# Weights loaded by halves of the heads and token transposes as column tiles, in a planned two-layer kernel

## The chip, the cores and the metric

The kernel runs on one core of one Trainium2 chip. The metric is the device time of one execution in microseconds. TensorE (PE in the profile) multiplies, ScalarE (ACT) does exponentials and copies, VectorE (DVE) does copies, statistics and a second kind of exponential, GpSimd (POOL) does small vector work, and SyncE (SP) issues the DMAs, all in one queue.

## The reference

Two blocks alternate, twice each, with the same weights: attention, then a mixer over the tokens.

```python
x = x + A(layernorm(x), wqkv, wo)            # 2048 tokens, width 640, 32 heads of 20
x = x + B(layernorm(x), w1, b1, w2, b2)      # a token MLP: 2048 -> 1536 -> 2048
x = x + A(layernorm(x), wqkv, wo)
x = x + B(layernorm(x), w1, b1, w2, b2)

def A(x, wqkv, wo):
    qkv = (x @ wqkv).reshape(B, S, 3, H, Dh).transpose(2, 0, 3, 1, 4)
    q, k, v = qkv[0], qkv[1], qkv[2]
    p = softmax(einsum("bhqd,bhkd->bhqk", q, k) * Dh ** -0.5)
    return einsum("bhqk,bhkd->bhqd", p, v).transpose(0, 2, 1, 3).reshape(B, S, D) @ wo

def B(x, w1, b1, w2, b2):
    u = gelu(einsum("bsd,sf->bdf", layernorm(x), w1) + b1)
    return (einsum("bdf,fs->bds", u, w2) + b2).transpose(0, 2, 1)
```

The layernorms have no learned scale. Inputs, weights and output are bfloat16.

## The kernel before

**Units of attention.** Heads are taken in 8 groups of four; a group's four heads sit at partitions 0, 32, 64 and 96 of the padded weights `wq` and `wk` (32 columns a head, 20 of them used), of `KT` (keys, transposed, 2048 columns a group) and of `QT` (512 queries of a group). A unit is one group, one block of 512 queries and one tile of 128 keys. Its scores are four matmuls that use 32 rows of the array each (`s_mms`, L700). ACT takes the exponential of two or three 512-column banks at once (L887, into `P`); for some units DVE does it instead with integer arithmetic (L840 and five passes of L860, into `JT`). The sums with V are matmuls with 32 columns of the array each, four side by side (L927, out of `P` or `JT`, with `Vaug`, which also holds a column of ones for the denominators).

**From x to Q, K and V.** `token_tile` takes one of 16 tiles of 128 tokens: statistics on DVE (L343 to L346), the scale on POOL (L354, L356), the normalised tile `h_bf` on DVE (L530, three buffers in the region of `attnT`), five 128x128 transposes on TensorE (L541, into a bfloat16 bank), and a copy into `hT` (region `hh`) by ACT or DVE (`copy`, L461 or L463). When four tiles are there, the projections of K and Q for 512 tokens can run (`add_proj`), and V's for each tile (`add_v`, half of the heads at a time). Every projection is a "fill": a list of matmuls that the planner puts between scores and sums. Outside attention these matmuls use the whole array (L453); within attention `mmul` issues each as four column tiles (L456), so that they stand next to the sums with V without a change of tiling. The transposes use the whole array at all times.

**Weights.** At the start `front` issues four token tiles, Q's weights, K's weights (800 KB each, region `JT`), two more token tiles, V's weights (800 KB, in the region `attnT`), and the other ten token tiles, for which eight slots exist. `pad_copies` spreads Q's and K's weights into the padded `wq` and `wk`, five copies of 128x640 each, on whichever of ACT and DVE is free. A projection may start when all five copies of its matrix are done. The second layer keeps `wq` and `wk` and loads V's weights again when the first layer's attention outputs are dead (`on_attnT_dead`).

**Order of attention.** The first layer takes groups 0 to 3 of the first 512 queries first, over key tiles 0 to 3 and then 4 to 15, as tokens come; then groups 4 to 7, then the other query blocks. The second layer takes key tiles four at a time, as the mixer of the first layer (`add_mm2`) gives out new tokens. The very last unit group (last query block, last head group) is taken in two halves of 256 queries, so that the output projection of the first half runs beside the second.

**Normalising.** After a group's sums are done, `normalize` turns them in 32x32 blocks on DVE (L977), takes reciprocals (L989), multiplies (L1000, on POOL, for the very last half on DVE) and turns them back (L1007). L1007 works on pairs of 16-bit values as 32-bit elements; the multiply writes the pairs in the order that needs, and `outproj` (L1059) reads its queries with the matching stride.

**The planner.** The whole program is one hand-written order. At build time the Python code simulates the five queues (`clk`) with estimated costs (`PE_MM`, 64 ns for a transpose, `PAD_V` for a pad copy on DVE, `DMA_RATE`, `SW` = 100 ns for a change of tiling on TensorE) and appends the cheapest ready instruction to each engine. The order on each engine is then fixed; on the chip semaphores keep it right, and an instruction that waits holds everything behind it on its engine. `fill_mode` tells the planner whether a fill runs in column tiles or on the whole array.

## Time and profile before

| what | value |
|---|---|
| median of 3 runs | 1728.17 us (1724.88 to 1728.33) |
| the profiled execution's own time | 1728.33 us |
| its span on the core | 1726.6 us |
| PE busy | 1643.3 us, 95% |
| ACT busy | 1583.5 us, 92% |
| DVE busy | 1458.4 us, 84% |
| POOL busy | 171.8 us, 10% |
| granted TensorE clock, mean | 0.997 |
| first layer's attention | 16 to 797 us |
| second layer's attention | 839 to 1652 us |

Times in the rows are in microseconds from the span's start, durations in microseconds on timeline rows and in nanoseconds for the mean of a group. A timeline row merges neighbours of one engine with the same line and tiles: start, length, engine, line, operation, written and read tiles, shape, how many, and in square brackets the idle time before it with what ended it. Matmuls are pipelined, so that a row of one matmul is longer than the distance to the next; distances between starts are what counts. `PEld` are weight loads. Lines named L461 and L463 belong to `copy`, L453 and L456 to `mmul` and L276 to `dma`, so their tiles tell which of them is meant.

### The profile page before, as it was taken

The page shows a single profiled execution, that of the slowest core. Times are in us where ns is not written, and L with a number is a line of the kernel's source. Part 1 is how long each engine was busy: PE and PEld are TensorE (multiplying, and loading weights), DVE is VectorE, ACT ScalarE, POOL GpSimd, SP SyncE. Part 2 cuts the span into 40 slices and gives each one's busy share as a digit, 9 for nine tenths or more (in the row PEclk, how much of TensorE's full clock was granted, in tenths as well). Part 3 has the DMA queues.
Part 4 walks back from the last instruction along what each step waited for, and adds up shares of the span by engine and source line. Part 5 has one row for each costly group of instructions (what it writes and reads, how often), then busy time and mean ns, then how long its engine had stood idle before and what let it go on. Part 6 is the DMA issues. An engine that isn't in the chain of part 4 may idle for free. (4 is left out here: it accounts for less than half of the span.)

```text
span 1726.6 us, 50507 instructions
## 1 busy us (share of the span) xinstructions
PE 1643.3 (95%) x21918; PEld 640.3 (37%) x21918; DVE 1458.4 (84%) x2620; ACT 1583.5 (92%) x1431; POOL 171.8 (10%) x260
## 2 busy tenths in 40 slices
PE   8999999999999999998999999999999999999989
PEld 3433333223333333335545432333333333332356
DVE  7688999999988898998444589999999889999973
ACT  8899999999999999997698899999999999999950
POOL 4000012000300020001101000100002000200010
PEclk9999999999999999999999999999999999999999
DMA  3200001000122016411521000100002120365142
GB/s 119 29 2 2 2 14 36 1 1 2 52 70 70 25 43 206 155 40 38 160 85 67 16 2 2 40 24 2 2 17 71 58 65 24 95 195 181 40 129 91
DMA packets 103294, 98.05 MB, mean 57 GB/s; under 512 B 45600, under 2 KB 79520, under 8 KB 103072
## 3 DMA queue, kind: packets, MB, share of 16 engines
q1 hardware_dynamic: 99456, 94.82, 17.8%
q8 instruction: 171, 2.80, 0.7%
q0 software_dynamic: 3616, 0.01, 0.3%
q14 instruction: 51, 0.42, 0.1%
HBM read 63.35 MB, written 31.46 MB: 55 GB/s over the span
## 5 line engine op out<-in xcount | busy, mean ns | idle before, releaser
L887 ACT ACTIVATE P<-pst 128x1536 bf16<-128x1536 f32 (+1 forms) x1337 | 1521.7, 1320 | 30.9 <-PE pst L700 17.0
L860 DVE TENSOR_SCALAR JT<-JT 128x2048 uint16<-128x2048 uint16 x945 | 633.9, 700 | 4.8 <-PE pst L927 1.6
L700 PE MATMUL pst<-QT,KT 32*128 32x512 bf16 (+1 forms) x4224 | 573.3, 376 | 44.5 <-ACT P L887 32.4
L840 DVE TENSOR_SCALAR JT<-pst 128x512 uint16<-128x512 f32 x756 | 504.2, 677 | 77.5 <-PE pst L700 75.8
L927 PE MATMUL pst<-P,Vaug 128*32 128x512 bf16 (+1 forms) x3444 | 509.1, 381 | 3.2 <-DVE T_85 L977 1.8
L927 PE MATMUL pst<-JT,Vaug 128*32 128x512 bf16 (+1 forms) x3900 | 470.8, 380 | 3.0 <-DVE T_85 L977 1.6
L700 PEld LDWEIGHTS <-KT 32*128 32x128 bf16 x4224 | 169.1, 91 | 515.7 <-issue 502.4
L927 PEld LDWEIGHTS <-Vaug 128*32 128x32 bf16 x7344 | 168.9, 94 | 295.2 <-issue 262.9
L1000 POOL TENSOR_TENSOR T_86<-T_85,rden 128x512 bf16<-128x512 f32 x64 | 67.7, 1059 | 1145.9 <-DVE rden L989 1106.1
L1481 PE MATMUL pst<-ident,zw 128*32 128x512 bf16 (+1 forms) x347 | 113.5, 380 | 0.0
L456 PEld LDWEIGHTS <-W 128*32 128x32 bf16 x3384 | 88.5, 96 | 64.6 <-issue 31.9
L1059 PE MATMUL pst<-wo,attnT 128*32 128x320 bf16 x2048 | 106.0, 301 | 3.9 <-DVE attnT L1007 2.9
L456 PE MATMUL pst<-hh,wq 128*32 128x512 bf16 x1232 | 104.6, 382 | 1.5 <-DVE JT L840 1.2
L456 PE MATMUL pst<-hh,wk 128*32 128x512 bf16 x1240 | 96.8, 381 | 1.3 <-DVE JT L840 0.6
L456 PE MATMUL pst<-x1last,W 128*32 128x320 bf16 x1536 | 78.9, 301 | 1.0 <-DVE W L1245 0.4
L1059 PEld LDWEIGHTS <-attnT 128*32 128x32 bf16 x2048 | 52.2, 96 | 38.8 <-issue 18.2
L456 PE MATMUL pst<-attnT,hh 128*32 128x320 bf16 x1196 | 60.2, 300 | 2.0 <-DVE hh L463 0.7
L456 PE MATMUL pst<-JT,W 128*32 128x320 bf16 x1080 | 52.3, 300 | 0.0
L463 DVE CAST KT<-pst 128x512 bf16<-128x512 f32 x52 | 35.3, 680 | 18.6 <-PE pst L456 18.4
L456 PE MATMUL pst<-hh,W 128*32 128x320 bf16 x768 | 42.8, 304 | 7.8 <-DMA W<-in_B_w_dram 4.5
L977 DVE STREAM_TRANSPOSE T_85<-pst 128x512 f32<-128x512 f32 (+1 forms) x58 | 40.0, 689 | 8.0 <-PE pst L927 7.9
L463 DVE CAST Vaug<-pst 128x320 bf16<-128x320 f32 x43 | 20.5, 482 | 30.4 <-PE pst L456 21.7
(91 smaller groups left out, 851.8 us busy)
## 6 DMA issues: line engine op xcount, KB each, us to landing
W<-in_B_w_dram SPq DMA_DIRECT2D x10, 768.0 KB
W<-in_B_w_dram SPq DMA_DIRECT2D x24, 256.0 KB
xs<-in_A_x_dram SPq DMA_DIRECT2D x32, 160.0 KB
x2d<-xs SPq DMA_DIRECT2D x16, 320.0 KB
xs<-x2d SPq DMA_DIRECT2D x16, 320.0 KB
x1d_69<-xs SPq DMA_DIRECT2D x12, 320.0 KB
uacca_72<-W SPq DMA_DIRECT2D x12, 320.0 KB
W<-uacca_72 SPq DMA_DIRECT2D x12, 320.0 KB
```

What stands on the lines that cost most here:

```text
L456: nc.tensor.matmul(out_[32 * c:32 * c + 32], lhsT=lhsT[:, 32 * c:32 * c + 32], rhs=rhs, start=start, stop=stop, tile_position=(0, 32 * c))
L463: nc.vector.tensor_copy(out=out_, in_=in_)
L700: pe(nc.tensor.matmul(dst, lhsT=k_, rhs=q_, start=True, stop=True, tile_position=(32 * j, 0)))
L840: nc.vector.tensor_scalar(out=c["jt"][:, j * 512:(j + 1) * 512], in0=Dt[:], scalar1=SCALE * LOG2E * 256.0, scalar2=127.0 * 256.0, op0=ALU. ...
L860: nc.vector.tensor_scalar(out=tt_[:], in0=c["jt"][:], scalar1=0.5, scalar2=TERM_C[i], op0=ALU.mult, op1=ALU.add)
L887: nc.scalar.activation(out=P[:, 0:n, :].rearrange("p a b -> p (a b)"), in_=St[:, 0:n, :].rearrange("p a b -> p (a b)"), func=ACT.Exp, scal ...
L927: pe(nc.tensor.matmul(dst, lhsT=Vaug[:, n:n + 32], rhs=ap, start=acc["cnt"][j] == 1 and not part, stop=last[j] and (half is None or part = ...
L977: nc.vector.transpose(out=T1[:], in_=src[:, 0:w])
L1000: eng.tensor_tensor(out=o_, in0=a_, in1=b_, op=ALU.mult)
L1059: nc.tensor.matmul(t[32 * c:32 * c + 32, 0:w], lhsT=q_, rhs=wo_pad[:, gg, c0:c1], start=(gi == 0), stop=(gi == len(gs) - 1), tile_position ...
L1481: pe(nc.tensor.matmul(dst[0:32, 0:128 * n], lhsT=zw[:, 0:32], rhs=ident[:].unsqueeze(1).to_broadcast([128, n, 128]), start=not inside, sto ...
```

## The change

- Q's, K's and V's weights are loaded in two halves, the first for heads 0 to 15 and the second for heads 16 to 31 (400 KB each, rows of 640 bytes). Q and K have four places in the region `JT`, V two in `attnT`. The first halves of Q and K are issued where the whole ones were, V's first half after token tile 5; the second halves get a lower priority on SP than token tiles that are ready.
- Q and K are padded by halves: 20 copies of 128x320 instead of 10 of 128x640. A projection waits for the half that its head group is in, and V's projection of one half for that half of V's weights. The second layer's V weights come in two loads as well.
- Within attention each transpose of a 128x128 block of normalised tokens becomes four, of 32 columns each, at column tiles 0, 32, 64 and 96. The planner treats them as column tiles.
- For the two halves of the last head group, the turning back works on 256 16-bit elements instead of 128 32-bit ones; the multiply writes in plain order, and the output projection of that group reads without the stride. All other groups stay as they were.
- Planner's costs: a pad copy on DVE 260 instead of 450, on ACT 460 instead of 730; the turning back 340 instead of 70 + 0.56 ns a query; the weight loads' rates.

```diff
-PAD_V = 450.0
+PAD_V = 260.0
...
-    at("wraw", "JT", 0, NDT * D * 2)
+    at("wraw", "JT", 0, NDT * D)
...
-    at("wv", "attnT", 0, NDT * D * 2)
+    at("wv", "attnT", 0, NDT * D)
...
-        return "col" if COL_FILL and not f["bf16"] and a is not None and a.want and not a.done else "full"
+        return "col" if COL_FILL and a is not None and a.want and not a.done else "full"
...
-            if t > start and t + f["cost"] + (SW if state.col or f["bf16"] else 0.0) > s_at[0] + FILL_OVER:
+            if t > start and t + f["cost"] + (SW if state.col else 0.0) > s_at[0] + FILL_OVER:
...
-        def load_wv():
-            L.wv = sb("wv", [128, NDT, D], BF16)
-            dma(L.wv[:], A_wqkv[:, 2 * D:3 * D].rearrange("(dt p) n -> p dt n", p=128), 128 * NDT * D * 2,
-                then=lambda t: setattr(L, "wv_ready", t))
+        def load_wv(hf):
+            L.wv[hf] = sb("wv", [128, NDT, D // 2], BF16, hf)
+            c0, c1 = COLS[hf]
+            dma(L.wv[hf][:], A_wqkv[:, 2 * D + c0:2 * D + c1].rearrange("(dt p) n -> p dt n", p=128), 64 * NDT * D * 2,
+                prio=1 + hf, rate=DMA_RATE * 0.8, then=lambda t: L.wv_ready.update({hf: t}))
...
-                        pe(nc.tensor.transpose(t[:, dt_, :], h_bf[:, dt_ * 128:(dt_ + 1) * 128], ident[:]))
+                        if state.col:
+                            for c in range(4):
+                                nc.tensor.transpose(t[32 * c:32 * c + 32, dt_, :], h_bf[:, dt_ * 128 + 32 * c:dt_ * 128 + 32 * c + 32], ident[:],
+                                                    tile_position=(0, 32 * c))
+                        else:
+                            nc.tensor.transpose(t[:, dt_, :], h_bf[:, dt_ * 128:(dt_ + 1) * 128], ident[:])
...
-            add_fill(mms, PE_MM, evac, 600.0, ready=ready, pr=pr, ok=lambda: w_left[what] == 0 and (what == "K" or len(rQ) > 0),
+            add_fill(mms, PE_MM, evac, 600.0, ready=ready, pr=pr, ok=lambda: w_left[(what, g // 4)] == 0 and (what == "K" or len(rQ) > 0),
...
-                            nc.vector.transpose(out=attnT[(qb, g)][:, q0:q1].bitcast(F32), in_=T2[:].rearrange("p c i -> p (c i)").bitcast(F32))
+                            o_, i_ = attnT[(qb, g)][:, q0:q1], T2[:].rearrange("p c i -> p (c i)")
+                            if half is None:
+                                o_, i_ = o_.bitcast(F32), i_.bitcast(F32)
+                            nc.vector.transpose(out=o_, in_=i_)
...
-            if L.nxt:
-                L.nxt.load_wv()
+            if L.nxt:
+                for hf in range(2):
+                    L.nxt.load_wv(hf)
...
-                copy(eng, w_view(wpad, dt_)[:, :, 0:DH], wr[:, dt_, :].rearrange("p (h i) -> p h i", i=DH))
+                copy(eng, w_view(wpad, dt_)[:, h0:h1, 0:DH], wr[:, dt_, :].rearrange("p (h i) -> p h i", i=DH))
...
-            either.append((1.5, t, seq[0], PAD_V, 730.0, f))
+            either.append((1.5 if hf == 0 else 2.5, t, seq[0], PAD_V, 460.0, f))
...
-        load_w(1)
-        load_w(0)
+        load_w(1, 0)
+        load_w(0, 0)
         for tt in range(4, 6):
             load_x0(tt)
-        L0.load_wv()
+        L0.load_wv(0)
         for tt in range(6, NT):
             load_x0(tt)
+        load_w(1, 1)
+        load_w(0, 1)
+        L0.load_wv(1)
```

## The prediction

> **What bounds the kernel now.** I read the page's first two parts, then the busy time in stretches of 20 us, then the timeline at three places: the first 17 us, the first layer's token stage to 80 us, and the second layer's token stage from 840 to 955 us. The page says that no engine is idle for long:
>
> ```profile
> PE 1643.3 (95%) x21918; PEld 640.3 (37%) x21918; DVE 1458.4 (84%) x2620; ACT 1583.5 (92%) x1431; POOL 171.8 (10%) x260
> L1481 PE MATMUL pst<-ident,zw 128*32 128x512 bf16 (+1 forms) x347 | 113.5, 380 | 0.0
> ```
>
> TensorE's 95% is an average with filler in it: L1481 is a matmul on zeros that only keeps the clock up, 113.5 us in all. Where those stand, TensorE has room; none stands between 16 and 40 us, and next to none in the second layer's token stage. So I look at the stages that the change touches one by one. First the start:
>
> ```profile
> 10.66 1.70 PE L453 MATMUL pst<-hh,wq 128*128 128x512 bf16 x7 [0.25 <-ACT hh L461]
> 9.29 0.72 ACT L461 COPY wq<-JT 128x640 bf16<-128x640 bf16 x1 [0.30 <-DMA JT<-in_A_wqkv_dram]
> 13.59 0.58 ACT L461 CAST KT<-pst 128x512 bf16<-128x512 f32 x1 [0.22 <-PE pst L453]
> 14.72 0.57 PE L453 MATMUL pst<-attnT,hh 128*128 128x320 bf16 x3 [1.17 <-DMA attnT<-in_A_wqkv_dram]
> 16.42 0.39 PE L700 MATMUL pst<-QT,KT 32*128 32x512 bf16 x3
> ```
>
> Q's weights land at about 9.2 us, but Q's projection starts at 10.66 when the fourth tile of normalised tokens is there. Keys are cast by 14.17. The first scores come only at 16.42: in TensorE's order a V projection stands ahead of them, and that one waits 1.17 us for V's weights, which land at 14.7.
>
> Then who waits for whom in the token stage of the first layer:
>
> ```profile
> 20.00:40.00 20.00, 19.13 (x257) 7.09 (x257) 14.96 (x37) 18.79 (x18) 6.82 (x14) 1.00 0.12 35
> 40.00:60.00 20.00, 19.66 (x282) 8.36 (x280) 9.62 (x21) 19.51 (x18) 4.59 (x3) 1.00 0.53 60
> 65.08 0.58 ACT L461 CAST KT<-pst 128x512 bf16<-128x512 f32 x1 [1.05 <-PE pst L456]
> 75.86 0.58 ACT L461 CAST KT<-pst 128x512 bf16<-128x512 f32 x1 [1.30 <-PE pst L456]
> ```
>
> The first two rows give PE, PEld, DVE, ACT, POOL. PE is full; ACT, which does the exponentials, catches up with the projections at 65 and 76 us and waits for keys. So this stage ends when TensorE's work ends, and what counts is TensorE's time, not ACT's first exponential. The second layer's token stage is the same: PE has 10.0 of 10 us from 840 to 860, and ACT waits 3.73 us at 908.9 and 3.94 us at 947.4 for the transposes of a new block of tokens. Their surroundings:
>
> ```profile
> 62.14 0.59 PE L456 MATMUL pst<-attnT,hh 128*32 128x320 bf16 x12
> 62.67 0.45 PE L541 MATMUL pst<-ident,attnT 128*128 128x128 bf16 x5
> 63.05 0.50 PE L927 MATMUL pst<-P,Vaug 128*32 128x512 bf16 x4
> 905.26 3.17 PE L456 MATMUL pst<-JT,W 128*32 128x320 bf16 x85
> 908.86 1.99 ACT L461 COPY hh<-pst 128x640 bf16<-128x640 bf16 x3 [3.73 <-PE pst L541]
> 912.91 1.26 PE L456 MATMUL pst<-hh,wk 128*32 128x512 bf16 x20
> ```
>
> Five whole-array transposes start (0.45-0.22)/4 = 0.057 us apart (one lasts 0.219). Going from column tiles into them costs about 0.53 - 3x0.137 = 0.12 us, leaving them about 0.38 - 5x0.057 = 0.095 us; 0.1 us a crossing.
>
> **Weights by halves (first layer).** Bytes come in order. Summing the DMA rates in half-microsecond slices from the start (56, 282, 300, 251, 274, 207, 177, 276, then some 364 GB/s), the 1,475 KB of four token tiles and Q's weights have moved at 7.0 us and are seen at 9.2: a lag of 2.2 us. By the same sums Q's half (1,065 KB) has moved at 5.9 and is seen at 8.1, K's half at 9.2 instead of 11.4, V's half (2,212 KB, two more token tiles before it) at 11.2 instead of 14.7. Rows of 640 bytes in place of 1,280 could slow this; the nearest row, w2's 512-byte rows at 344 to 351 GB/s from 1652 to 1660 us, makes it 5%, V's half at 11.5. It is then there before TensorE asks for it at 13.4: minus 1.17 us. ACT's pad copies of Q come ahead of its copies of the transposed tokens, for the half now lands as ACT is done with its memsets (8.13): four copies of 320 columns at 0.43 (the 128x320 cast's row) where one of 0.72 stood, which I take to delay the last token copy by 0.3 us; against it, TensorE's waits for wq copies of 0.28 and 0.22 us go. Taken: minus 1.2 us. Bounds: 0, if another wait, for the token copies, fills the hole; minus 2.25, if the first scores follow the key cast at once (16.42 - 14.17).
>
> The second halves: ten more pad copies, 0.16 to 0.32 us each on DVE (row: 0.32 for 640 columns), 2 to 3 us that fall on DVE between 15 and 60 us, where it is busy under 75%; on ACT they would be ten times 0.43. Cover gone, they cost ACT's share, 2 us. SP issues three more DMAs, 0.5 us each (two took 1.00). Ahead of token tile 8 stand 3,280 KiB instead of 3,680 KiB, so no token comes later; its issue waits for a free slot till 7.5 us anyway. POOL's queue is not touched. In the second layer V's load is issued at 799.60 and first used at 828.5: one more issue of 0.38 us on a queue that next issues at 818.7. Nothing.
>
> **Transposes as column tiles.** 120 of the 160 transposes lie within attention, 60 in each layer, in pieces between other matmuls. Counting pieces that follow or precede column-tile matmuls without another wait between, I find 12 crossings in the first layer and 8 in the second: 20x0.1 = minus 2.0 us, all in stages where TensorE is the bound. The row that the trace does not have is four transposes of 32 columns side by side with 128 moving columns. Column-tile groups of four run 0.137 us apart at 320 columns and (1.26-0.38)/4 = 0.22 at 512: both give 0.055 at 128 in proportion, which is also the whole-array row. I take 0.057: no change. The other end is that a group never goes faster than at 320 columns: 120x(0.137-0.057) = plus 9.6 us. That bound also holds for 480 instructions in place of 120, should their issue set the pace.
>
> A rule of the Trainium skill speaks against this edit. TensorEngine Tiling (Array Packing), "Restrictions" under Tile-to-Partition Mapping, says that column tiling disables the fast weight load, and TensorE: Matmul & The Clock Gate, "LDWEIGHTS (loading the stationary operand)", puts a load at columns/1.2 ns. An estimate from that page is 107 ns for four loads of 32 columns, and with it this term would be plus 4.0 us instead of minus 2.0; no row of this trace shows loads as the limit.
>
> **The last head group in 16-bit elements.** The second halves' transposes (L1007, 0.31 us for 128x128 32-bit) are on the path at both layers' ends; 128x256 16-bit elements cost between 0.31 and the 0.43 of the 128x256 32-bit row. Taken 0.43: 2x0.12 = plus 0.25 us, bounds 0 and 0.25. The multiply ahead of it keeps its 256 elements (0.44). The first halves lie beside POOL and other head groups.
>
> **Planner's costs** (PAD_V, 340 for the turning back) move the order, not the work.
>
> Sum: -1.2 - 2.0 + 0.25 = -2.95. The profiled execution took 1728.33 us (span 1726.6), 0.16 above the median of 1728.17: 1725.4.
>
> **Rivals.**
> 1. Slower: column-tile transposes are paced by their instructions or weight loads, not by 128 columns. For: 8 instructions a group, a pace that the trace never shows. Against: at 512 and 320 columns the pace is proportional. At 0.137 us a group the time is 1725.4 + 9.6 = 1735.0; from 0.11 us on it is over 0.2% slower than before.
> 2. Nothing reaches the end: TensorE's order has other waits (0.59 us at 18.7 for a V cast, ACT's casts at 65) that take up the gains, and only the +0.25 is left: 1728.6. Against: PE is full in the windows.
> 3. A larger gain: the new order also brings one of the two token blocks in time (the 3.73 us wait), and the start keeps 2.25 instead of 1.2: 1725.4 - 3.7 - 1.0 = 1720.7. For: the waits are just after TensorE's full stretch. The same re-planning the other way, one wait more, gives 1729.2, with a second 1733.
>
> **How the numbers follow.** Forecast 0.38, its own range 1723.5 to 1727.5; larger gain 0.23; nothing reaches the end 0.10; slow tiles 0.20; a worse order 0.09. About 0.2%, 3.5 us, is what a measurement of this kernel can tell from no change, so faster means under 1724.7 and slower over 1731.6. Two fifths of the forecast's chance (0.15) and the larger gain are faster: 0.38. Nearly all of the slow tiles (0.19) and over half of the worse order (0.06) are slower: 0.25. Same has the other 0.37. The range runs from the larger gain to the milder slow tiles and the worse order: 1720.5 to 1733.
>
> **What would show it.** First V projection without a wait on its weights and first scores near 15.2 us; ACT's key waits near 65 and 76 us about 2 us earlier; column-tile transposes with starts of groups 0.055 to 0.06 us apart and no 0.1 us before them; total TensorE busy time about the same. Wrong if groups are over 0.08 us apart, if token copies move past 11 us, or if the ACT waits at 909 and 947 change by more than 1 us either way.

## The result: 7.7 us faster, and the profile after

The changed kernel took 1720.34 us (median of 4 executions, 1718.20 to 1722.07) against 1728.03 us before (median of 4, 1724.88 to 1728.33). The ratio is 0.9959 with a 95% interval from 0.9942 to 0.9976: faster, by 7.7 us. The forecast was 1725.4 us, so the sign was right and the size 2.6 times what was expected; 1720.34 lies 0.2 us below the stated range of 1720.5 to 1733. As the experiments show, the gain doesn't come from where the forecast put it.

The page of the changed kernel begins like that of before. The columns are busy time, share of the span and number of instructions of each engine, and for groups of instructions: line, engine, operation and count, then busy time and mean ns of one, then idle time ahead of the group and what ended most of it. The line numbers are some 8 to 16 higher than before.

```profile
span 1718.9 us, 51196 instructions
...
PE 1645.1 (96%) x22256; PEld 642.6 (37%) x22256; DVE 1465.9 (85%) x2635; ACT 1580.4 (92%) x1433; POOL 167.4 (10%) x260
...
L895 ACT ACTIVATE P<-pst 128x1536 bf16<-128x1536 f32 (+1 forms) x1335 | 1519.9, 1310 | 29.3 <-PE pst L708 15.6
L848 DVE TENSOR_SCALAR JT<-pst 128x512 uint16<-128x512 f32 x760 | 506.8, 678 | 66.0 <-PE pst L708 63.7
...
L1497 PE MATMUL pst<-ident,zw 128*32 128x512 bf16 (+1 forms) x333 | 109.1, 379 | 0.0
```

TensorE is busy 1.8 us longer in a span that is 7.7 us shorter, although 14 of the filler matmuls on zeros (L1497) are gone, so TensorE doesn't have less to do. ACT's busy time falls by 3.1 us and DVE's rises by 7.5. The granted clock isn't what makes the kernel faster: its mean in the profiled execution is 0.994, against 0.997 before. (TensorE's count rises by 338; with 360 instructions more for the transposes and 14 fillers fewer, little else is left.) The question is where the time went.

**The start.** A timeline has the start of a run of instructions, its length, the instructions with their count, and in brackets the idle time ahead of it and what ended it. The last copy of transposed tokens that Q needs was, before:

```profile
9.92 0.69 ACT L461 COPY hh<-pst 128x640 bf16<-128x640 bf16 x1
```

This is the changed kernel's first 16 us:

```profile
8.04 1.88 ACT L462 COPY wq<-JT 128x320 bf16<-128x320 bf16 x5
9.82 1.53 ACT L462 COPY wk<-JT 128x320 bf16<-128x320 bf16 x4
10.36 2.31 PE L454 MATMUL pst<-attnT,hh 128*128 128x320 bf16 x8
11.26 0.68 ACT L462 COPY hh<-pst 128x640 bf16<-128x640 bf16 x1
12.49 1.25 PE L454 MATMUL pst<-hh,wq 128*128 128x512 bf16 x5
13.58 1.24 PE L454 MATMUL pst<-hh,wk 128*128 128x512 bf16 x5
15.82 0.60 PE L708 MATMUL pst<-QT,KT 32*128 32x512 bf16 x5
```

V's projection (`attnT,hh`, 10.36) no longer waits for its weights; the wait of 1.17 us is gone, and the planner put V ahead of Q. But Q's projection began at 12.49 where it began at 10.66 before. ACT padded Q's half from 8.04 on and most of K's from 9.82 on, and copied the last token tile only at 11.26, 1.3 us later than before; Q can't begin before that copy ends at 11.94. The rest of Q's delay goes with the clock. From 10 to 12 us TensorE was granted half of it in this execution (a row of these gives the stretch, its length, the busy time of PE, PEld, DVE, ACT and POOL with their instructions, the granted clock, the DMA share and GB/s):

```profile
10.00:11.00 1.00, 1.00 (x8) 0.77 (x7) 0.97 (x4) 1.00 (x4) 0.00 (x0) 0.50 1.11 330
11.00:12.00 1.00, 1.00 (x6) 0.54 (x5) 0.97 (x4) 1.00 (x3) 0.74 (x2) 0.50 1.16 303
```

Before had 1.00 in the same two stretches. V's eight matmuls started 0.267 us apart here, and 0.136 apart in the five at 14.66, at a clock of 1.00. The first scores come at 15.82 instead of 16.42.

**The transposes.** The second layer's token stage, TensorE alone; the third line is the same 20 instructions taken together (shortest, median and longest duration in ns, first and last start):

```profile
905.70 1.54 PE L457 MATMUL pst<-attnT,hh 128*32 128x320 bf16 x39
907.08 0.46 PE L546 MATMUL pst<-ident,attnT 128*32 128x128 bf16 x20
...
L546 PE MATMUL pst<-ident,attnT x20: 216/219/230, 907.1 to 907.3; 128*32 128x128 bf16 x20
```

Twenty transposes are five groups of four. The groups start 0.055 us apart (907.079, 907.134, 907.189, 907.244 and 907.299 in the single records), as whole-array transposes did. The last group of the projection ahead of them started at 905.70 + 1.54 - 0.30 = 906.94, so 0.14 us before: the ordinary distance of column-tile groups at 320 columns. The crossing of about 0.1 us is gone.

**The waits of ACT in the second layer.** ACT does most of the exponentials, so its waits for scores and sums show where attention stands still. The answer lists what ACT waited for between 960 and 1650 us: total, times, longest. Before:

```profile
ACT P L887 <- PE pst L927: 8.0, 8, 3.2
ACT P L887 <- PE pst L700: 5.0, 13, 0.9
```

and after:

```profile
ACT P L895 <- PE pst L935: 6.5, 12, 2.8
ACT P L895 <- PE pst L708: 3.5, 10, 0.9
```

Together 13.0 us before and 10.0 us after. No edit of the change touches the order of this stretch directly: there are no weights to load in it and no token transposes. That pointed to the planner.

**Where the 7.7 us went, by stages.** To place the difference I counted the 4,096 exponential chunks of 512 columns in the records of ACT and DVE and took the time at which the k-th is done. The profiled executions (1728.33 and 1720.68 us) differ by:

| stage | before, us | after less before, us |
|---|---|---|
| start to first chunk | 18.34 | -0.6 |
| chunk 1 to 120, first layer's token stage | 61.02 | -0.25 |
| 120 to 512 | 155.66 | -3.05 |
| 512 to 2048, end of the first layer's attention | 561.38 | +1.3 |
| 2048 to 2260, mixer and second token stage | 169.16 | -1.9 |
| 2260 to 4090, rest of the second layer | 683.67 | -3.1 |
| to the end | 77.35 | -0.1 |

The first row says little: between executions whose order at the start is the same, the first chunk comes from 0.4 us earlier to 1.1 us later (c_cost -0.4, c_layout +0.5, b_emit +1.0 and c_330 +1.1, below, against before). Later stages move too: c_only and c_cost, below, have the same order, and their stages differ by up to 1.6 us.

### The profile page after: what moved, and what is told of

It reads as the page before. It is cut to its first block, busy times and chain, and to the rows that moved or that the text cites. A ratio compares the mean times of both kernels' runs of the same rounds, so it can differ in the third digit from the quotient of the medians.

```text
span 1718.9 us, 51196 instructions
## 1 busy us (share of the span) xinstructions
PE 1645.1 (96%) x22256; PEld 642.6 (37%) x22256; DVE 1465.9 (85%) x2635; ACT 1580.4 (92%) x1433; POOL 167.4 (10%) x260
## 5 line engine op out<-in xcount | busy, mean ns | idle before, releaser
L935 PE MATMUL pst<-P,Vaug 128*32 128x512 bf16 (+1 forms) x3440 | 501.8, 381 | 3.9 <-DVE T_85 L985 1.8
L1074 PE MATMUL pst<-wo,attnT 128*32 128x320 bf16 x2048 | 111.5, 301 | 5.9 <-DVE attnT L1020 3.3
L1497 PE MATMUL pst<-ident,zw 128*32 128x512 bf16 (+1 forms) x333 | 109.1, 379 | 0.0
L464 DVE CAST QT<-pst 128x512 bf16<-128x512 f32 x59 | 39.5, 669 | 9.0 <-PE pst L457 8.8
L355 POOL TENSOR_SCALAR rt<-mv 128x1 f32<-128x1 f32 x64 | 13.5, 210 | 343.9 <-DVE mv L347 343.7
```

The source lines that it names most:

```text
L464: nc.vector.tensor_copy(out=out_, in_=in_)
L935: pe(nc.tensor.matmul(dst, lhsT=Vaug[:, n:n + 32], rhs=ap, start=acc["cnt"][j] == 1 and not part, stop=last[j] and (half is None or part = ...
L1074: nc.tensor.matmul(t[32 * c:32 * c + 32, 0:w], lhsT=q_, rhs=wo_pad[:, gg, c0:c1], start=(gi == 0), stop=(gi == len(gs) - 1), tile_position ...
L1497: pe(nc.tensor.matmul(dst[0:32, 0:128 * n], lhsT=zw[:, 0:32], rhs=ident[:].unsqueeze(1).to_broadcast([128, n, 128]), start=not inside, sto ...
```

## The experiments

Twelve kernels ran. All of them compute the whole reference. Each was timed against the kernel before on the same chip; the ratios have 95% intervals. 0.0010 is 1.7 us.

| kernel | edit to the kernel before | median, us | before on the same chip, us | ratio |
|---|---|---|---|---|
| a_only | weights by halves | 1731.48 | 1729.06 | 1.0016 [1.0007, 1.0025] |
| b_only | transposes as column tiles | 1730.33 | 1729.06 | 1.0006 [0.9997, 1.0015] |
| c_only | turning back: 16-bit halves and cost of 340 | 1722.43 | 1729.06 | 0.9962 [0.9949, 0.9975] |
| ab | both of the first two | 1727.72 | 1729.06 | 0.9995 [0.9986, 1.0004] |
| b_emit | column-tile transposes in before's order | 1728.33 | 1728.78 | 0.9999 [0.9990, 1.0009] |
| b_plan | only the planner's view of the transposes | 1727.03 | 1728.78 | 0.9992 [0.9983, 1.0000] |
| c_layout | only the 16-bit halves | 1727.77 | 1728.78 | 0.9994 [0.9985, 1.0002] |
| c_cost | only the cost of 340 | 1722.30 | 1728.78 | 0.9957 [0.9945, 0.9969] |
| c_330 | only the cost, 330 | 1719.88 | 1728.34 | 0.9950 [0.9938, 0.9961] |
| c_350 | only the cost, 350 | 1722.01 | 1728.34 | 0.9965 [0.9952, 0.9978] |
| c_true | only the cost, 430 and 310 | 1722.44 | 1728.34 | 0.9965 [0.9952, 0.9978] |
| ab_cost | a, b and the cost of 340 | 1721.95 | 1728.34 | 0.9965 [0.9952, 0.9979] |

### One part at a time: a_only, b_only, c_only, ab

The first four take the change apart. `a_only` has the loads and pad copies by halves, with their planner's costs:

```diff
-PAD_V = 450.0
+PAD_V = 260.0
...
-        load_w(1)
-        load_w(0)
+        load_w(1, 0)
+        load_w(0, 0)
...
-        L0.load_wv()
+        L0.load_wv(0)
...
+        load_w(1, 1)
+        load_w(0, 1)
+        L0.load_wv(1)
```

> The kernel before with only the weights loaded and padded by halves (and the pad copies' costs in the planner). The whole change gave 1728.0 to 1720.3 us, -7.7. Theory 1 (work: each part is worth what it saves in its own stage): the first layer's token stage ends 0.9 us earlier, as in the changed kernel, and the time falls by 1 us, to 1727. Theory 2 (order: a part is worth mostly what the planner makes of the later units when anything shifts): the token stage ends within 1 us of before, and the time differs from that by 2 us or more, either way.

Alone, part A is slower, by 1.2 to 4.3 us. The start did what the change says: V's projection ran at 10.77 and the first scores came at 15.32. What was won there was lost again in the first token stage. ACT's timeline of a_only:

```profile
67.07 0.59 ACT L462 CAST KT<-pst 128x512 bf16<-128x512 f32 x1 [1.99 <-PE pst L457]
...
77.92 0.59 ACT L462 CAST KT<-pst 128x512 bf16<-128x512 f32 x1 [1.30 <-PE pst L457]
```

Before, the two keys' casts stood at 65.08, after a wait of 1.05 us, and at 75.86: the keys come 2 us later instead of earlier, and by the count of chunks this stage is 3.2 us longer. (This profiled execution took 1728.36 us, less than its kernel's median, so the stages of a_only don't add up to its median loss.) A part of that loss can be the clock: over all executions on record, taken kernel by kernel, a mean granted clock lower by 0.001 goes with about 0.9 us more, and a_only's mean is 0.9940, against 0.9950 for before on its chip. An estimate from these is 0.9 of the 2.4 us by which the medians differ.

`b_only` has the transposes as column tiles and the planner's view of them:

```diff
-        return "col" if COL_FILL and not f["bf16"] and a is not None and a.want and not a.done else "full"
+        return "col" if COL_FILL and a is not None and a.want and not a.done else "full"
...
-            if t > start and t + f["cost"] + (SW if state.col or f["bf16"] else 0.0) > s_at[0] + FILL_OVER:
+            if t > start and t + f["cost"] + (SW if state.col else 0.0) > s_at[0] + FILL_OVER:
...
-                        pe(nc.tensor.transpose(t[:, dt_, :], h_bf[:, dt_ * 128:(dt_ + 1) * 128], ident[:]))
+                        if state.col:
+                            for c in range(4):
+                                nc.tensor.transpose(t[32 * c:32 * c + 32, dt_, :], h_bf[:, dt_ * 128 + 32 * c:dt_ * 128 + 32 * c + 32], ident[:],
+                                                    tile_position=(0, 32 * c))
+                        else:
+                            nc.tensor.transpose(t[:, dt_, :], h_bf[:, dt_ * 128:(dt_ + 1) * 128], ident[:])
```

> The kernel before with only the transposes as column tiles within attention, in the plan and on the chip. Theory 1 (work): about 20 crossings of 0.1 us are saved, -2 us, to 1726, half in each layer's token stage. Theory 2 (order): the token stages shorten by that much or less, and the time differs from -2 us by 2 us or more, through the order of the units between 80 and 790 us and after 960 us.

No difference that can be told from none, and the forecast's minus 2.0 us (a ratio of 0.9988) lies outside the interval.

`c_only` has the third part, the 16-bit turning back of the last group's halves and the planner's new cost of turning back:

```diff
-                            nc.vector.transpose(out=attnT[(qb, g)][:, q0:q1].bitcast(F32), in_=T2[:].rearrange("p c i -> p (c i)").bitcast(F32))
-                            end = start + 70 + 0.56 * w
-                            rT2.give(s2, end)
-                            on_normal(qb, g, half, end + LAT_V)
-                        push("DVE", 0 if half is not None else 3, end_, 70 + 0.56 * w, f_tr2, ok=lambda: len(rA) > 0 and L.v_left[1] == 0)
+                            o_, i_ = attnT[(qb, g)][:, q0:q1], T2[:].rearrange("p c i -> p (c i)")
+                            if half is None:
+                                o_, i_ = o_.bitcast(F32), i_.bitcast(F32)
+                            nc.vector.transpose(out=o_, in_=i_)
+                            rT2.give(s2, start + 340)
+                            on_normal(qb, g, half, start + 340 + LAT_V)
+                        push("DVE", 0 if half is not None else 3, end_, 340, f_tr2, ok=lambda: len(rA) > 0 and L.v_left[1] == 0)
```

> The kernel before with only the last head group's halves turned as 16-bit elements and 340 ns as the planner's cost of turning back. Theory 1 (work): +0.25 us at most, 1728.2. Theory 2 (order): the cost of 340 instead of 357 ns stands 62 times in the plan and moves the order: up to 4 us either way.

This part alone gives 0.9962, nearly all of the gain. `ab` is the changed kernel with this part taken out:

```diff
 # the changed kernel, with:
-                            rT2.give(s2, start + 340)
-                            on_normal(qb, g, half, start + 340 + LAT_V)
-                        push("DVE", 0 if half is not None else 3, end_, 340, f_tr2, ok=lambda: len(rA) > 0 and L.v_left[1] == 0)
+                            end = start + 70 + 0.56 * w
+                            rT2.give(s2, end)
+                            on_normal(qb, g, half, end + LAT_V)
+                        push("DVE", 0 if half is not None else 3, end_, 70 + 0.56 * w, f_tr2, ok=lambda: len(rA) > 0 and L.v_left[1] == 0)
...
 # and the multiply, the turning back and outproj's stride as before
```

> The changed kernel with the last head group's halves turned as 32-bit pairs, as before. Theory 1 (work): 0.25 us faster than the changed kernel, 1720.1. Theory 2 (order): as the planner's cost of turning back differs from the changed kernel's, the time may be up to 4 us away from 1720.3, and the sum of the three single changes need not give it.

A and B together: minus 0.9 us, not told from nothing. A's loss in the token stage is not there: with B beside it, the cast of keys that stood at 67.07 in a_only is earlier. ACT's timeline of ab:

```profile
66.29 0.59 ACT L462 CAST KT<-pst 128x512 bf16<-128x512 f32 x1 [0.93 <-PE pst L457]
```

So the effect of A on that stage depends on what stands around it; whether the other order or the column tiles bring the cast forward wasn't separated. What ACT waited for in ab between 960 and 1650 us is as before the change, 12.5 us together:

```profile
ACT P L895 <- PE pst L935: 8.3, 9, 3.2
ACT P L895 <- PE pst L708: 4.2, 12, 0.9
```

### The instructions without the plan, and the plan without the instructions: b_emit, b_plan, c_layout, c_cost

Parts B and C each hold two things: other instructions, and another number for the planner, after which it finds another order. The next four separate these. In `b_emit` the planner counts as before, so that the order is before's, and only each transpose is issued as four:

```diff
-                        pe(nc.tensor.transpose(t[:, dt_, :], h_bf[:, dt_ * 128:(dt_ + 1) * 128], ident[:]))
+                        if COL_FILL and state.att is not None and state.att.want and not state.att.done:
+                            for c in range(4):
+                                nc.tensor.transpose(t[32 * c:32 * c + 32, dt_, :], h_bf[:, dt_ * 128 + 32 * c:dt_ * 128 + 32 * c + 32], ident[:],
+                                                    tile_position=(0, 32 * c))
+                        else:
+                            nc.tensor.transpose(t[:, dt_, :], h_bf[:, dt_ * 128:(dt_ + 1) * 128], ident[:])
```

> The kernel before with its order of instructions unchanged on every engine, where only each of the 120 whole-array transposes within attention is issued as four column tiles. This is the edit's work without its re-planning. Theory 1 (work): 20 crossings of 0.1 us in stages where TensorE is the bound: 1.5 to 2 us faster, 1726. Theory 2 (order): under 1 us, since an order planned around the crossings has its other waits where they were.

0.9999: the saved crossings don't reach the end. The stage with the first layer's 60 transposes is 0.5 us shorter, and the mixer stage 0.9 us, but the latter hangs on a transfer. Ahead of the attention of the second layer, where the transposes are on the whole array in both kernels, TensorE waited 1.43 us for a normalised tile in before's profiled execution:

```profile
833.39 0.45 PE L541 MATMUL pst<-ident,attnT 128*128 128x128 bf16 x5 [1.43 <-DVE attnT L530]
```

and 0.23 us in b_emit's:

```profile
833.06 0.45 PE L546 MATMUL pst<-ident,attnT 128*128 128x128 bf16 x5 [0.23 <-DVE attnT L530]
```

The work and the order there are the same. What DVE, which makes the tile, waited for between 826 and 836 us has this row in before (total, times, longest) and none for a DMA in b_emit:

```profile
DVE xs L1389 <- DMA x2d<-xs: 1.9, 1, 1.9
```

So the difference is when a transfer landed in one execution and in the other. Whether the edit has a part in that isn't shown: c_layout, also in before's order, has the wait as before does (1.80 us for the same transfer, 1.29 us for TensorE).

`b_plan` is the other half: the planner counts column tiles, the chip gets whole-array transposes.

```diff
-        return "col" if COL_FILL and not f["bf16"] and a is not None and a.want and not a.done else "full"
+        return "col" if COL_FILL and a is not None and a.want and not a.done else "full"
...
-            if t > start and t + f["cost"] + (SW if state.col or f["bf16"] else 0.0) > s_at[0] + FILL_OVER:
+            if t > start and t + f["cost"] + (SW if state.col else 0.0) > s_at[0] + FILL_OVER:
```

> The reverse: the planner counts the transposes as column tiles (no 0.1 us for a change of tiling), so that the order is that of the column-tile kernel, but the chip does whole-array transposes. Theory 1 (work): 2 us slower than the kernel with both, about as fast as before. Theory 2 (order): most of what the kernel with both gains is kept.

0.9992, with an interval that ends at 1.0000: at most a small gain, though the order is quite another (a comparison of the two lists of some 43,800 matmuls and weight loads on TensorE gives 11,000 lines of difference). A new order alone need not change the time.

`c_layout` has the 16-bit halves with the old costs; the orders of TensorE, ACT and SP are those of before:

```diff
-                            nc.vector.transpose(out=attnT[(qb, g)][:, q0:q1].bitcast(F32), in_=T2[:].rearrange("p c i -> p (c i)").bitcast(F32))
+                            o_, i_ = attnT[(qb, g)][:, q0:q1], T2[:].rearrange("p c i -> p (c i)")
+                            if half is None:
+                                o_, i_ = o_.bitcast(F32), i_.bitcast(F32)
+                            nc.vector.transpose(out=o_, in_=i_)
...
-                        q_ = at_[:].rearrange("p (c i b) -> p c b i", b=2, i=32)[:, n // 2, n % 2]
+                        if qb == LASTQB and gg == NG - 1:
+                            q_ = at_[:, 32 * n:32 * n + 32]
+                        else:
+                            q_ = at_[:].rearrange("p (c i b) -> p c b i", b=2, i=32)[:, n // 2, n % 2]
```

> The kernel before with its order unchanged, where only the last head group's halves are turned as 256 16-bit elements (0.31 to 0.43 us an instruction, two on the path). Both theories: 0 to 0.25 us slower. The rows of the turning back settle its price.

No difference (0.9994). The groups of c_layout show the new turning back beside that of whole groups, four of them at 439 ns:

```profile
L1012 DVE STREAM_TRANSPOSE attnT<-T 128x256 f32<-128x256 f32 x62 | 26.5, 429 | 1.8 <-POOL T L1002 1.8
...
L1012 DVE STREAM_TRANSPOSE attnT<-T 128x256 bf16<-128x256 bf16 x4 | 1.8, 439 | 0.1
```

`c_cost` changes one number. The planner counts 340 ns for every turning back, in place of 70 + 0.56 x 512 = 357 for a whole group and 70 + 0.56 x 256 = 213 for a half. No instruction is of another kind or size:

```diff
-                            end = start + 70 + 0.56 * w
+                            end = start + 340
                             rT2.give(s2, end)
                             on_normal(qb, g, half, end + LAT_V)
-                        push("DVE", 0 if half is not None else 3, end_, 70 + 0.56 * w, f_tr2, ok=lambda: len(rA) > 0 and L.v_left[1] == 0)
+                        push("DVE", 0 if half is not None else 3, end_, 340, f_tr2, ok=lambda: len(rA) > 0 and L.v_left[1] == 0)
```

> The kernel before with one number of the planner changed: turning back costs 340 instead of 357 ns (340 instead of 213 for the two halves). Every instruction does what it did; the order alone moves. Theory 1 (work): within 0.5 us of before. Theory 2 (order): 2 us or more away from before, either way.

0.9957 [0.9945, 0.9969]: this one number gives as much as the whole change, whose ratio is 0.9959 [0.9942, 0.9976]. c_only has the same order on every engine, with the 16-bit halves in it, and 0.9962.

Up to the 120th chunk the stages of c_cost and before agree to 0.01 us but for the start; from there on the orders part, and some 13,700 lines of TensorE's list differ. By the same count of chunks c_cost wins 1.6 us from chunk 120 to 512, gives 1.35 us back until the end of the first layer, and wins 5.3 us from chunk 2260 to 4090. In c_only, in the same order, these are 3.05 us won, 2.8 lost and 3.7 won, so single stages of one execution are good to some 1.5 us. ACT's waits between 960 and 1650 us in c_cost, 7.6 us together in place of 13.0 (9.3 in c_only):

```profile
ACT P L887 <- PE pst L927: 4.6, 11, 1.3
ACT P L887 <- PE pst L700: 3.0, 9, 0.9
```

One place shows what kind of wait that is. ACT's timeline of before, between 1455 and 1600 us, only the runs that begin after a wait of over 0.8 us:

```profile
1487.46 3.28 ACT L887 ACTIVATE P<-pst 128x1024 bf16<-128x1024 f32 x3 [3.21 <-PE pst L927]
...
1542.73 42.00 ACT L887 ACTIVATE P<-pst 128x1024 bf16<-128x1024 f32 x37 [0.89 <-PE pst L700]
...
1587.23 13.71 ACT L887 ACTIVATE P<-pst 128x1536 bf16<-128x1536 f32 x12 [2.50 <-PE pst L927]
```

c_cost in the same window has one such wait:

```profile
1581.03 19.58 ACT L887 ACTIVATE P<-pst 128x1536 bf16<-128x1536 f32 x17 [1.26 <-PE pst L927]
```

TensorE of before, ahead of 1487.46:

```profile
1484.18 0.86 PE L1059 MATMUL pst<-wo,attnT 128*32 128x320 bf16 x20
1484.98 0.39 PE L700 MATMUL pst<-QT,KT 32*128 32x512 bf16 x3
1485.30 0.40 PE L927 MATMUL pst<-JT,Vaug 128*32 128x512 bf16 x4
1485.53 1.40 PE L1059 MATMUL pst<-wo,attnT 128*32 128x320 bf16 x36
1486.97 0.62 PE L927 MATMUL pst<-P,Vaug 128*32 128x512 bf16 x8
```

ACT has nothing to do from 1484.25 on. What lets it go on comes with the eight sums at 1486.97, and TensorE's order has 20 and 36 matmuls of the output projection ahead of them, 2.26 us, which the planner had put there as fills. TensorE is busy all the while, so its 95% doesn't show that attention stands. c_cost has no such stop between 1469 and 1581 us. The last wait, 2.50 us before and 1.26 in c_cost, goes with a lower clock: TensorE's granted clock is 0.57 from 1584 to 1588 us in before, and 1.00 from 1576 to 1584 in c_cost.

A second thing moved with the number. The planner shares the exponentials out between ACT and DVE, four chunks of 512 columns to a unit, and the group of DVE's first pass counts them; ACT's group has the other chunks. Before:

```profile
L887 ACT ACTIVATE P<-pst 128x1536 bf16<-128x1536 f32 (+1 forms) x1337 | 1521.7, 1320 | 30.9 <-PE pst L700 17.0
L840 DVE TENSOR_SCALAR JT<-pst 128x512 uint16<-128x512 f32 x756 | 504.2, 677 | 77.5 <-PE pst L700 75.8
```

and in c_cost:

```profile
L840 DVE TENSOR_SCALAR JT<-pst 128x512 uint16<-128x512 f32 x760 | 506.6, 678 | 63.9 <-PE pst L700 61.6
```

One unit more goes to DVE. ACT's 1521.7 us are for the other 3,340 chunks, 0.456 us each, so that is 4 x 0.456 = 1.8 us less for ACT. With the 5.4 us less of waits from 960 us on this makes 7.2 us, of the same size as the 6.5 us by which the medians differ; the first layer's two differences, minus 1.6 and plus 1.35 us, nearly cancel.

### Is it the direction, the truth of the number, or any other order? c_330, c_350, c_true, ab_cost

The rest asks why 340 is better than 357. Three readings were open: a smaller number is better; a truer number is better (the chip takes 430 for a whole group and 310 for a half); or any number gives another order, with a gain or loss by chance. Each kernel changes the same two places as c_cost. `c_330`:

```diff
-                            end = start + 70 + 0.56 * w
+                            end = start + (330.0 if half is None else 330.0)
...
-                        push("DVE", 0 if half is not None else 3, end_, 70 + 0.56 * w, f_tr2, ok=lambda: len(rA) > 0 and L.v_left[1] == 0)
+                        push("DVE", 0 if half is not None else 3, end_, (330.0 if half is None else 330.0), f_tr2, ok=lambda: len(rA) > 0 and L.v_left[1] == 0)
```

> The kernel before with the planner's cost of turning back at 330 ns, where 357 (213 for the halves) gave 1728.8 and 340 gave 1722.3. Theory order-by-chance (any number gives another order, good or bad): anywhere between 1722 and 1733, not tied to 1722. Theory direction (a lower cost makes a better plan): at or below 1722.

`c_350` has 350 in both places:

```diff
+                            end = start + 350.0
...
+                        push("DVE", 0 if half is not None else 3, end_, 350.0, f_tr2, ok=lambda: len(rA) > 0 and L.v_left[1] == 0)
```

> The same at 350 ns, nearer to the kernel before than 340. Theory order-by-chance: anywhere between 1722 and 1733. Theory direction: between 1722 and 1728.8, about 1726.

`c_true` has the measured durations:

```diff
+                            end = start + (430.0 if half is None else 310.0)
...
+                        push("DVE", 0 if half is not None else 3, end_, (430.0 if half is None else 310.0), f_tr2, ok=lambda: len(rA) > 0 and L.v_left[1] == 0)
```

> The same at 430 ns for whole groups and 310 for the halves, what the instructions take in the profile (429 and 306). Theory order-by-chance: anywhere between 1722 and 1733. Theory direction: slower than before, 1731 or more. A third theory, that a truer cost makes a better plan: 1726 or less.

All three are faster than before, 0.9950, 0.9965 and 0.9965, and with c_cost their medians lie within 1719.9 to 1722.4 us. So for whole groups the direction is out, since 430 and 330 both win. That truth is what counts is out for them too: 330 is further from 430 than 357 is, and it has the lowest median of all. (For the halves all four numbers are larger and truer than 213; see below.) Chance of either sign fits badly as well, as seven kernels with a new number (these four, c_only, ab_cost and the changed kernel) are all faster by 5.9 to 8.5 us, while the six that keep the old formula (a_only, b_only, ab, b_plan and, in before's own order, b_emit and c_layout) lie between minus 1.8 and plus 2.4 us by their medians. But these are fewer orders than kernels: c_only has c_cost's, ab_cost the changed kernel's and b_plan b_only's, so five new orders win and three others don't. Nor is it the clock: the seven have means of 0.9926 to 0.9957 of granted clock, before 0.9949 to 0.9952 on the three chips, which at 0.9 us for 0.001 is under 1 us.

Nor is it one wait. c_350 keeps the stop at the group's end, and is as fast as c_cost:

```profile
1487.68 46.27 ACT L887 ACTIVATE P<-pst 128x1024 bf16<-128x1024 f32 x41 [3.77 <-PE pst L927]
1534.12 67.25 ACT L887 ACTIVATE P<-pst 128x1536 bf16<-128x1536 f32 x59 [0.16 <-PE pst L927]
```

It has no other wait of over 0.4 us from there to the end of the window. What these kernels share are two sums. The first is ACT's waits for TensorE's scores and sums (the two rows shown) from 960 to 1650 us: 7.6 us in c_cost, 9.3 in c_only, 9.2 in c_350, 10.2 in c_330, 7.5 in c_true, 9.7 in ab_cost and 10.0 in the changed kernel, against 12.5 to 13.6 in before and in all six kernels with the old formula. The second is the count of chunks on DVE: 764 in c_350, 760 in the six other kernels with a new number, and 756 or 752 in all with the old formula. c_330, the fastest, has these waits, and 4.4 us of its gain lie in the first layer, between chunks 120 and 2048:

```profile
ACT P L887 <- PE pst L927: 6.4, 10, 2.2
ACT P L887 <- PE pst L700: 3.8, 10, 0.9
```

`ab_cost` is the changed kernel with the halves turned back as before, in 32-bit pairs, but at the planner's cost of 340. TensorE's order is the changed kernel's:

```diff
 # the changed kernel, with:
-                            o_, i_ = attnT[(qb, g)][:, q0:q1], T2[:].rearrange("p c i -> p (c i)")
-                            if half is None:
-                                o_, i_ = o_.bitcast(F32), i_.bitcast(F32)
-                            nc.vector.transpose(out=o_, in_=i_)
+                            nc.vector.transpose(out=attnT[(qb, g)][:, q0:q1].bitcast(F32), in_=T2[:].rearrange("p c i -> p (c i)").bitcast(F32))
...
-                        if qb == LASTQB and gg == NG - 1:
-                            q_ = at_[:, 32 * n:32 * n + 32]
-                        else:
-                            q_ = at_[:].rearrange("p (c i b) -> p c b i", b=2, i=32)[:, n // 2, n % 2]
+                        q_ = at_[:].rearrange("p (c i b) -> p c b i", b=2, i=32)[:, n // 2, n % 2]
```

> The changed kernel, with its order on every engine as far as the two layouts allow, but the last head group's halves turned as 32-bit pairs: weights by halves, column-tile transposes and the planner's cost of 340. It is the one with all three that may beat both kernels. By the order: 1720 to 1722, as the changed kernel, and up to 0.25 us less for the shorter turning back; if the 16-bit layout itself brought the gain, 1727.7 as with the two other edits alone.

0.9965 [0.9952, 0.9979], against 0.9995 for ab, which differs from it by the number alone. Its stages follow the changed kernel's within 0.4 us throughout. The 16-bit layout adds nothing that can be told.

**What stays open.** Why the old formula gives the slower orders isn't settled. Five numbers were run and four of them win, by different waits in different places. That less work for ACT and fewer stops make the time is read from the profiles of one execution each; no kernel moved a unit to DVE and did nothing else. Each new number also changed what the halves are counted at (213 to 310 or more), and a kernel with 340 for whole groups and 213 for halves wasn't run. Built without running, its order of TensorE differs from c_cost's in 110 lines, before's in some 13,900; the reverse, 357 for whole groups and 340 for the halves, leaves ACT's order as before's and TensorE's too up to the end of the first layer, where the halves first come. Both speak for the whole groups' number, but that is argued, not measured. The fastest kernel here, c_330, is the kernel before with one number changed; its interval overlaps that of the changed kernel, and the two weren't run side by side.

## Why the prediction was right in its sign and wrong in its reasons

The forecast's reasons are not what made the gain. That the sign came out right is luck, since the two terms that carried it gave nothing that can be told from zero. (The sum starts from the profiled execution, 1728.33 us; from before's median of 1728.17 it gives 1725.2, not 1725.4.)

**The step that failed** is the one of a single sentence: "Planner's costs (PAD_V, 340 for the turning back) move the order, not the work." It was costed at nothing. The sentence is true but for one unit that went from ACT to DVE. What it leaves out is that the order is worth 5 to 8.5 us: c_cost 0.9957, and the medians of ab_cost and ab, each taken against before on its chip, are 5.1 us apart (minus 6.4 and minus 1.3). I named neither the work that would hide a change of order nor its price if nothing did. The page gave 30.9 us of idle time ahead of ACT's exponentials, and 13.0 of them lie between 960 and 1650 us, a stretch that was not looked at, for no edit seemed to touch it.

**Weights by halves, minus 1.2 us.** The first sign came true: V's projection doesn't wait. The second, first scores near 15.2, came as 15.32 in a_only and 15.82 in the changed kernel. The third, the waits for keys near 65 and 76 us about 2 us earlier, did not: the casts stand at 65.10 and 74.98 in the changed kernel, 0.0 and 0.9 us from before, and 2 us later in a_only. Alone the part costs 1.2 to 4.3 us. The term that was mis-sized is the delay of the last token copy, taken as 0.3 us for Q's pad copies alone: four of K's now stand ahead of it as well, and it came 1.3 us later, at 11.26. That is the forecast's own sign of being wrong, token copies past 11 us. The step took the wait out of a fixed order, and the planner found another.

**Column tiles, minus 2.0 us.** The two terms were right on the spot, 0.055 us a group (taken 0.057) and no crossing, but the sum wasn't seen: b_emit, which saves every crossing in the old order, is at 0.9999, and 2.0 us would have been 0.9988, outside its interval. What was missing is the step from TensorE's time in a stage to the end. The forecast took TensorE to be the bound in the token stages because it is full there; the stage itself gave 0.5 us in the first layer, and no run puts more than that down to the edit.

The rule that the forecast weighed against this edit can now be set beside a row. By the Trainium skill, TensorEngine Tiling (Array Packing), "Restrictions", column tiling loses the fast weight load, and TensorE: Matmul & The Clock Gate, "LDWEIGHTS (loading the stationary operand)", gives a load a time by its columns, from which 107 ns a group was estimated. The groups run at 55 ns, and b_emit isn't slower. Here the measurement decides: the slow-tiles rival is out.

**Turning back, plus 0.25 us.** Its term was right, 0.437 us in the changed kernel where 0.31 stood before; c_layout (minus 2.6 to plus 0.3 us by its interval) can't tell 0.25 from nothing.

**The rivals.** The third, "a larger gain", gave 1720.7 us, and 1720.34 was measured; it was also the one that named re-planning. But its place was wrong. It wanted one of the two token blocks in time. ACT's timeline of the changed kernel there:

```profile
904.11 1.53 ACT L462 COPY hh<-pst 128x640 bf16<-128x640 bf16 x2 [2.67 <-PE pst L546]
...
942.79 1.53 ACT L462 COPY hh<-pst 128x640 bf16<-128x640 bf16 x2 [3.85 <-PE pst L546]
```

The waits were 3.73 and 3.94 us before; neither went. The first changed by 1.06 us, just past the 1 us that the forecast gave as a sign of being wrong. From the last exponential ahead of each block to the first behind it, ACT's gap was 10.23 and 10.44 us and is now 9.35 and 10.53. The agreement with 1720.7 is by the number alone. The mirror of this rival, a worse order, may be what a_only shows, though its clock has a part in that.

So the forecast's sum, minus 2.95 us, consists of terms of which A and B together gave minus 0.9 us, not told from zero, and the fourth, taken as zero, gave nearly all.

## What to carry to other kernels

Where a program finds its own order from estimated costs, every number in it is an edit of its own, and can be worth more than the instructions that it stands for: here one number, 357 to 330, 340, 350 or 430, was worth 6 to 8.5 us, and two edits that save waits and crossings on the spot under one. Take such a change apart in both directions, the new instructions in the old order and the new order with the old instructions, before a gain is put down to what the instructions do. And a gain of this kind belongs to the order that it was measured in. Here it lasted when A and B were added (c_only 0.9962, the changed kernel 0.9959); that the next edit leaves it isn't shown.

## What the runs showed of the hardware

Transposes of 128x128 16-bit values as four column tiles of 32 columns run at 55 ns a group of four, the same as one whole-array transpose, with 360 more instructions and 360 more weight loads in the kernel at no measurable cost (b_emit, 0.9999). Executions of the same order differ in when the first exponential is done (from 0.4 us earlier to 1.1 us later than before) and in single stages (by up to 1.6 us between c_only and c_cost); a single profiled execution can't place a difference smaller than that. A part of this is the granted clock, which falls to 0.5 for stretches of some 3.4 or 6.8 us, at other times in each execution: none before 16 us in before, 9.1 to 12.5 us in the changed kernel, 8.4 to 15.3 in b_emit.
